# Single units at both ends of a fused recurrence and feed-forward: new weight pieces, output turns by transfer, and a re-planned order

## Chip, cores and metric

The kernel runs on one core of one Trainium2 chip. The metric is device time in microseconds (us). The comparison value is the median of several executions; one further execution was recorded by the hardware profiler, and its page and trace are what is read below. Engines: PE (TensorE), its weight loads (PEld), DVE (VectorE), ACT (ScalarE), POOL (GpSimd) and SP (SyncE, which only issues transfers).

## What is computed

```python
# q, k, v, alpha: (B=4, H=8, S=768, D=48) float32
for t in range(S):                       # one state per batch and head
    state = alpha[:, :, t, :, None] * state + einsum('bhd,bhe->bhde', k[:, :, t], v[:, :, t])
    y[:, :, t] = einsum('bhd,bhde->bhe', q[:, :, t], state)
x = y.transpose(0, 2, 1, 3).reshape(B * S, H * D)          # 3072 x 384
h = maximum(maximum(x @ w1, x @ w2), x @ w3)               # 3072 x 768
out = h @ w_out                                            # 3072 x 384
```

The setup draws alpha from 0.8 to 1.0.

## The kernel before, in words

The 768 positions are cut into 6 chunks of 128, and with 4 batches this gives 24 **units** (chunk, batch) of 128 positions and 8 heads; unit u is chunk u // 4, batch u % 4. Two neighbouring units are a **group** n; group n holds units 2n and 2n+1. The loads of q, k, v and alpha bring one tensor of one unit (192 KB) in the first four groups, later one tensor of a whole group (384 KB), into five rotating buffers each.

*Attention of one unit* (`decay`, `prep`, `output`, `state`): ACT takes the logarithm of alpha (L498). PE sums it along the chunk (L551, "cums") and forms the totals of the group (L511). ACT exponentiates with both signs (L554, L556). q and k are multiplied with these (L563) and v is scaled (L569 on ACT, L574 on POOL); the table EARLY names the engine of each of the three for some units, and POOL takes them for the rest. PE turns the products by 8 transposes (L533, "turn-in") and DVE copies them out (L537, tile qkT); from unit CROSS_IN on a transposing transfer on the SP queue does both (L581). PE makes the scores (L596), DVE masks them (L601, tile LA), PE makes the outputs (L639 with the carried state, L642 with the scores), ACT scales them (L650, tile xb). Three transposes (L664) and a copy (L668) give the turned output xT, or, from unit CROSS_OUT on, one transposing transfer on SP (L656; no unit has one before, since CROSS_OUT is 24). From unit PAIRS on the scores of two units are issued together. The state moves on by L694 (PE), L700 (DVE) and L707 (POOL, in the first chunk DVE).

*Feed-forward* (`ffn`): since max(a, b, c) = a + max(0, b - a, c - a), the kernel holds the differences w2 - w1 and w3 - w1 (tile wd, indexed by g = 0, 1; made by the subtractions of `subs`, L446) and the product w1 @ w_out (tile w1o; `turned`, L463, turns w1, and `folded`, L480, multiplies). A call serves two units. Six pieces of two 128-column blocks each are made for g = 0 and for g = 1 alternately: 6 matmuls of 256 columns (L735), then ACT's relu for g = 0 (L746) or DVE's maximum for g = 1 (L751), both into hT. Then "shrink" (L768), 9 matmuls of 384 columns for each unit: 3 of xT with w1o and 6 of hT with w_out. ACT copies the result out and issues the store (L779, L780).

*Weights* (`wload`) come over the SP queue in two pieces of 384 columns each (WCUTS); w1 and w_out are cast by ACT (L437). In the list FIRST, which fixes the order of the first transfers, ("w", g, p) is piece p of w1, w2, w3, w_out for g = 0, 1, 2, 3, and ("aq", n, 0, 1) the first unit of group n for alpha and q.

*Order.* The whole order is planned while the kernel is built. Each step has an engine, a cost, a rank and the tiles that it reads and writes. `Plan.order` takes again and again the step that can begin first, with ties by rank; it models the transfers (`Transfers`), PE's clock (`Clock`) and the eight PSUM banks. The instructions are emitted in that order, so each engine's queue is fixed before the run. The ranks of the feed-forward are its first unit plus LEAD. `warm` puts in matmuls of zeros (L676) at the lowest rank, which start behind one product of one unit (WARM).

Of the kernel before, what the change touches and what calls it, by code (L numbers as in the profile page):

```python
# [24 lines left out]
SP_FIRST = 0.9  # L25
QUEUES = ("SP", "POOL")
DMA_IN = {"SP": 0.9, "POOL": 2.7}
DMA_OUT = {"SP": 0.9, "POOL": 0.9}
DMA_BOTH = {"SP": 0.2, "POOL": 0.85}
SPARE = 1.5  # L30
LEAD = (6.0, 9.0, 7.0)
EARLY = {1: ("POOL", "DVE", "POOL"), 3: ("DVE", "DVE", "POOL"), 4: ("POOL", "POOL", "POOL"),
         5: ("DVE", "POOL", "POOL"), 6: ("DVE", "DVE", "POOL"), 7: ("POOL", "DVE", "POOL"),
         8: ("POOL", "DVE", "ACT"), 9: ("POOL", "DVE", "ACT"), 10: ("POOL", "DVE", "ACT"),
         11: ("POOL", "POOL", "POOL")}
WEIGHTS = ()
WCUTS = (0, 384, 768)
SUBS = {(1, 0): "DVE", (1, 1): "DVE", (2, 0): "DVE", (2, 1): "DVE"}
FIRST = (("aq", 0, 0, 1), ("aq", 0, 1, 2), ("k", 0, 1, 2), ("w", 0, 0), ("v", 1, 0, 1),
         ("k", 0, 0, 1), ("k", 1, 0, 1), ("w", 0, 1), ("qa", 1, 0, 1), ("w", 1, 1),  # L40
         ("w", 1, 0), ("v", 0, 0, 1), ("v", 0, 1, 2), ("k", 1, 1, 2), ("a", 1, 1, 2),
         ("w", 3, 1), ("q", 1, 1, 2), ("w", 3, 0), ("w", 2, 0), ("v", 1, 1, 2), ("w", 2, 1),
         ("aqkv", 2, 0, 2), ("a", 3, 0, 1), ("a", 3, 1, 2), ("qk", 3, 0, 1), ("v", 3, 0, 1),
         ("k", 3, 1, 2), ("q", 3, 1, 2), ("v", 3, 1, 2))
WARM = (0, 0, 12)
PAIRS, WIDE = 12, 99
CROSS_IN, CROSS_OUT = 21, 24
FETCH, FETCHES, STORE = 1.0, (24.5, 11.0), 0.3
CLOCK_WINDOW, CLOCK_PHASE, CLOCK_WAKE, CLOCK_KEEP = 3.413, 0.0, 0.75, 0.37

# [70 lines left out]
class Plan:  # L121
# [55 lines left out]
    def order(self):  # L177
# [16 lines left out]
        for i in range(n):  # L194
            if not waiting[i]:
                ready[i] = 0.0
                pending[self.steps[i][0]].add(i)
        free = dict(dict.fromkeys(HOP, 0.0), SP=SP_FIRST)
        bank_free = {b: 0.0 for b in range(NBANKS)}
        place, seq, clock = {}, [], Clock()  # L200
# [18 lines left out]
        while len(seq) < n:  # L219
            best = None  # L220
            for e, cand in pending.items():
                pick = None
                for i in cand:
                    at = self.homes(bank_free, self.steps[i][5])
                    if at is None:
                        continue
                    t = max(ready[i], free[e], at[0])
                    turn = TURN_RANK if e == "PE" and self.steps[i][7] != mode else 0.0
                    key = (t, self.steps[i][2] + turn, i)
                    if pick is None or key < pick:  # L230
                        pick = key
                if pick is not None and (best is None or pick < best[0]):
                    best = (pick, e)
# [4 lines left out]
            if landing and (best is None or landing[0] <= best[0][0]):  # L238
                end, i = dma.next(commit=True)
                self.landed[i] = end  # L240
                finish(i, end)
                continue
# [7 lines left out]
            if e == "PE":  # L250
# [3 lines left out]
                cost = clock.run(t, cost)  # L254
            free[e] = t + cost
            seq.append((t, i))
            if load and e in QUEUES:
                dma.add(e, t + cost + DMA_IN[e], load, i, late)
            else:
                if load:  # L260
                    dma.store(load)
                finish(i, t + cost + HOP[e])
# [7 lines left out]
def kernel(  # L270
# [111 lines left out]
    def banks2(key, dtype):  # L382
# [7 lines left out]
             (("a", alpha), ("q", q), ("k", k), ("v", v))}  # L390

    def load(n, lo, hi, names="aqkv"):
        cb, g = divmod(n, B // UB)
        for x in names:
            t = ld[x][n % 5]

            def run(x=x, t=t):
                nc.sync.dma_start(  # L398
                    t[:, lo:hi],
                    views[x][cb * P:(cb + 1) * P, g * HG + lo:g * HG + hi])  # L400

            plan.step("SP", 0.5, -1.0, run, line="loads",
                      writes=[(x, n % 5, h) for h in range(lo // H, hi // H)],
                      load=1.82 * (hi - lo) / HG,
                      late=0.0 if n < 3 else SPARE)

    nparts = len(WCUTS) - 1
    matrices = (moe_w1, moe_w2, moe_w3, moe_w_out)
    casting = {g: tuple(x[2] for x in FIRST if x[:2] == ("w", g)) for g in (0, 3)}

    def weights(g, gate):
        plan.step("POOL", 0.78, -1.0,
                  lambda: nc.gpsimd.dma_start((w1h, 0, 0, wo16)[g],
                                              matrices[g].rearrange("(t p) f -> p t f", p=P)),
                  reads=[gate], writes=[("w", g, p) for p in range(nparts)], line="weights",
                  load=3.2 if g == 0 else 4.1)
        if g == 0:
            turned()
        else:
            folded()  # L420

# [4 lines left out]
    def wload(g, part):  # L426
        plan.step("SP", 0.5, -1.0,
                  lambda: nc.sync.dma_start(  # L428
                      piece(wst[g], g, part),
                      piece(matrices[g].rearrange("(t p) f -> p t f", p=P), g, part)),  # L430
                  reads=[("ws room", p) for p in casting[0]] if g == 3 else [],
                  writes=[("ws", g, part)], line="loads",
                  load=3.25 * (WCUTS[part + 1] - WCUTS[part]) / DF)
        if g in (0, 3):
# [7 lines left out]
    def subs(g, part):  # L442
# [3 lines left out]
                  lambda: (nc.gpsimd if eng == "POOL" else nc.vector).tensor_sub(  # L446
                      wd[:, :, g - 1, cols], wst[g][:, :, cols], w1h[:, :, cols]),
                  reads=[("ws", g, part), ("w", 0, part)], writes=[("wd", g, part)])

# [41 lines left out]
    def decay(n):  # L491
# [28 lines left out]
        if cb > 0:  # L520
            m = n - B // UB
            plan.step("DVE", 0.45, 2 * n + 0.5,
                      lambda: nc.vector.tensor_mul(Gs[m % 3], e12s[m % 4][:, :, 1],
                                                   e12s[n % 4][:, :, 0]),
                      reads=[("e", m % 4), ("e", n % 4)], writes=[("G", m % 3)])

# [13 lines left out]
    def prep(u):  # L540
# [11 lines left out]

        plan.step("PE", 0.17, u, cums, banks=[Lk], reads=[("la", n % 3, i)], writes=[Lk])
        plan.step("ACT", 0.49, u, lambda: nc.scalar.activation(out=ep, in_=live[Lk], func=AFT.Exp),  # L554
# [4 lines left out]
        for w, x, e in ((0, "q", ep), (1, "k", en)):  # L559
# [3 lines left out]
                          nc.gpsimd if eng == "POOL" else nc.vector).tensor_mul(  # L563
                              qk[:, w, :, :D], ld[x][n % 5][:, hs], e),
                      reads=[(x, n % 5, i), ("ep" if w == 0 else "en", u % 3)],
                      writes=[("qk", u % 7, w)])
# [61 lines left out]
    def output(u):  # L628
# [6 lines left out]
        def outs():  # L635
            yp = live[yk] = bank(yk, [P, H, D], FP32)
            for j in range(NP):
# [3 lines left out]
                for p in range(2):  # L641
                    nc.tensor.matmul(yp[:, 2 * j + p, :], LA[:, p, j, :], v16[:, 2 * j + p, :],  # L642
                                     start=(cb == 0), stop=True, skip_group_check=True)

        plan.step("PE", 0.38 if cb else 0.21, u, outs, banks=[yk], writes=[yk],
                  reads=[("qkT", u % 3), ("LA", u % 3), ("v16", u % 7), ("qkT room", u % 3),
# [18 lines left out]

        plan.step("PE", 0.17, u, turn, banks=[xk], reads=[("xb", u % 5)], writes=[xk])
        plan.step("DVE", 0.35, u,
# [48 lines left out]
    def ffn(f, units):  # L716
# [3 lines left out]
        xT, hT = xTs[c][:, :, base * P:(base + k) * P], hTs[f % 3]  # L720
        span = 4 // k
        npieces = 2 * (NJ // span) + k
        rank = [u0 + LEAD[min(f, 2)] + k * i / npieces for i in range(npieces)]
        for q in range(NJ // span):
            js = range(q * span, (q + 1) * span)
            parts = sorted({p for j in js for p in parts_of(j // 2)})
            for g in range(2):
# [3 lines left out]
                def grow(js=js, g=g, gk=gk):  # L731
                    live[gk] = bank(gk, [P, span, k * P], FP32)
                    for jj, j in enumerate(js):
                        for kt in range(NFT):
                            nc.tensor.matmul(live[gk][:, jj, :], wd[:, kt, g, j * P:(j + 1) * P],  # L735
                                             xT[:, kt, :], start=(kt == 0), stop=(kt == NFT - 1))

                plan.step("PE", 0.656 if span > 1 else 0.643, r, grow, banks=[gk],
                          writes=[gk] + [("room", f % 3, j) for j in js] * (g == 0),
# [4 lines left out]
                if g == 0:  # L744
                    plan.step("ACT", 0.59, r,
                              lambda h=h, gk=gk: nc.scalar.activation(out=h, in_=live[gk],  # L746
                                                                      func=AFT.Relu),
                              reads=[gk], writes=[("hT", f % 3, j) for j in js])
                else:
                    plan.step("DVE", 0.69, r,  # L750
                              lambda h=h, gk=gk: nc.vector.tensor_max(h, live[gk], h),  # L751
                              reads=[gk] + [("hT", f % 3, j) for j in js],
                              writes=[("hT", f % 3, j) for j in js])
        for i in range(k):
# [4 lines left out]
            nk = NFT + NJ  # L759
            parts = [(0, nk)] if m < NU - UB else [(0, nk - 2), (nk - 2, nk)]  # L760
            for lo, hi in parts:
# [19 lines left out]

            plan.step("ACT", 0.86, r, leave, reads=[ok], writes=[("ob room", m % 4)], load=STORE)

# [12 lines left out]
    for n in range(NU // B):  # L796
        us = list(range(n * B, (n + 1) * B))
        due += [us] if n >= WIDE else [us[:UB], us[UB:]]
    nf = len(due)
    for n in range(NG):  # L800
# [6 lines left out]
        for u in range(n * UB, (n + 1) * UB):  # L807
# [3 lines left out]
            if u == WARM[0]:  # L811
                warm(*WARM)
            for g, after, x in WEIGHTS:
                if after == u:
                    weights(g, ("v16", u % 7) if x == "v" else ("qk", u % 7, "qk".index(x)))
            for v in (u - 1, u) if u >= PAIRS else (u,):
# [44 lines left out]
```

## Time and profile before

| what | before |
|---|---|
| median of 3 runs (lowest, highest) | 156.61 us (156.6, 157.32) |
| profiled execution: its time, its span | 157.07 us, 155.3 us |
| PE, PEld busy | 138.2 us (89%), 105.8 us (68%) |
| DVE, ACT, POOL busy | 100.6 us (65%), 86.5 us (56%), 67.2 us (43%) |
| read from HBM, written | 23.69 MB, 4.72 MB |
| last group's load issued | at 109.58 us |
| last matmul ends | at about 151.0 us |

The span runs from the first to the last recorded event; the run's own time is 1.77 us longer. Busy times of PE are unions of records whose ends are modelled and overlap, so PE's backlog is counted below by numbers of matmuls and their spacing in the chain of waits. The columns of that chain are: start in us, length in us, what it was.

### The profile page before, as it was taken

The page shows a single profiled execution, that of the slowest core. Times are in us where ns is not written, and L with a number is a line of the kernel's source. Part 1 is how long each engine was busy: PE and PEld are TensorE (multiplying, and loading weights), DVE is VectorE, ACT ScalarE, POOL GpSimd, SP SyncE. Part 2 cuts the span into 40 slices and gives each one's busy share as a digit, 9 for nine tenths or more (in the row PEclk, how much of TensorE's full clock was granted, in tenths as well). Part 3 has the DMA queues.
Part 4 walks back from the last instruction along what each step waited for, and adds up shares of the span by engine and source line. Part 5 has one row for each costly group of instructions (what it writes and reads, how often), then busy time and mean ns, then how long its engine had stood idle before and what let it go on. Part 6 is the DMA issues. An engine that isn't in the chain of part 4 may idle for free.

```text
span 155.3 us, 4013 instructions
## 1 busy us (share of the span) xinstructions
PE 138.2 (89%) x1600; PEld 105.8 (68%) x1600; DVE 100.6 (65%) x171; ACT 86.5 (56%) x173; POOL 67.2 (43%) x95
## 2 busy tenths in 40 slices
PE   0578537999998999999999999999999999999990
PEld 0244425757777967798778688878797787868750
DVE  7044756398599997669768869958684752923220
ACT  3734707747547666496768284848575462535221
POOL 0332190011912154076999749999858600000000
PEclk9999999999999999999999999999999999999999
DMA  6999999999999999999999999999894232011202
GB/s 123 227 240 253 325 209 344 330 181 232 207 243 219 180 239 246 211 269 189 231 219 207 222 253 231 180 243 267 195 202 86 101 72 77 24 55 51 83 18 101
DMA packets 109394, 29.45 MB, mean 190 GB/s; under 512 B 103104, under 2 KB 109376, under 8 KB 109376
## 3 DMA queue, kind: packets, MB, share of 16 engines
q1 hardware_dynamic: 105632, 24.38, 75.4%
q10 hardware_dynamic: 3744, 4.82, 9.1%
q8 instruction: 12, 0.20, 0.5%
q14 instruction: 6, 0.05, 0.1%
HBM read 23.69 MB, written 4.72 MB: 183 GB/s over the span
## 4 chain that ended last, share of the span: by engine, by line
PE 76%; SPq 6%; issue 4%; DVE 4%; DMA 3%; POOL 2%; ACT 2%; ACTq 0%; POOLq 0%
PE psum L735 30%; PE psum L768 23%; PE psum L533 5%; SPq L398 5%; PE psum L596 4%; DMA qn<-in_q_dram 3%; PE psum L642 3%; PE psum L639 2%; POOL qk L563 2%; PE psum L551 2%; PE psum L664 2%; PE psum L480 2%; PE psum L694 2%; DVE LA L601 2%; SPq L428 1%
## 5 line engine op out<-in xcount | busy, mean ns | idle before, releaser
L735 PE MATMUL psum<-xT,wd 128*128 128x256 f16 x432 | 55.7, 276 | 0.2
L735 PEld LDWEIGHTS <-wd 128*128 128x128 f16 x432 | 41.0, 99 | 7.1 <-issue 0.5
L563 POOL TENSOR_TENSOR qk<-qn,ep 128x384 f16<-128x384 f32 x21 | 21.5, 1028 | 37.5 <-ACT ep L554 29.7
L751 DVE TENSOR_TENSOR hT<-psum,hT 128x512 f16<-128x512 f32 x36 | 24.2, 686 | 16.0 <-PE psum L735 12.1
L601 DVE TENSOR_TENSOR LA<-psum,c 128x1024 f16<-128x1024 f32 x24 | 28.6, 1216 | 7.0 <-PE psum L596 7.0
L746 ACT ACTIVATE hT<-psum 128x512 f16<-128x512 f32 x36 | 21.5, 605 | 17.2 <-PE psum L735 16.9
L768 PE MATMUL psum<-wo,hT 128*128 128x384 f16 x144 | 27.3, 326 | 0.0
L779 ACT COPY ob<-psum 128x384 f32<-128x384 f32 x24 | 11.5, 478 | 23.2 <-PE psum L768 22.8
L768 PEld LDWEIGHTS <-hT 128*128 128x128 f16 x144 | 14.1, 98 | 9.3
L650 ACT ACTIVATE xb<-psum,c 128x384 f16<-128x384 f32 x24 | 13.9, 582 | 10.7 <-PE psum L642 9.6
L574 POOL TENSOR_SCALAR v<-vn,c 128x384 f16<-128x384 f32 x21 | 12.6, 601 | 13.7 <-DMA vn<-in_v_dram 13.5
L563 POOL TENSOR_TENSOR qk<-kn,en 128x384 f16<-128x384 f32 x17 | 18.4, 1087 | 0.2 <-DMA kn<-in_k_dram 0.2
L537 DVE COPY qkT<-psum 128x1024 f16<-128x1024 f16 x21 | 14.2, 685 | 5.7 <-PE psum L533 5.0
L533 PE MATMUL psum<-c,qk 128*128 128x128 f16 x168 | 14.5, 232 | 3.8 <-POOL qk L563 3.7
L707 POOL TENSOR_TENSOR Z<-U,G 48x192 f16<-48x192 f32 x32 | 15.7, 504 | 3.9 <-DVE U L700 2.8
L768 PE MATMUL psum<-w1o,xT 128*128 128x384 f16 x72 | 15.7, 326 | 0.0
L533 PEld LDWEIGHTS <-qk 128*128 128x128 f16 x168 | 11.2, 104 | 5.7 <-POOL qk L563 4.6
L554 ACT ACTIVATE ep<-psum 128x384 f32<-128x384 f32 x24 | 11.9, 495 | 2.8 <-PE psum L551 2.7
L668 DVE COPY xT<-psum 128x384 f16<-128x384 f16 x24 | 8.3, 352 | 7.7 <-PE psum L664 6.5
L551 PE MATMUL psum<-la,c 128*128 128x384 f16 x24 | 8.5, 354 | 4.5 <-ACT la L498 4.5
L498 ACT ACTIVATE la<-an 128x768 f16<-128x768 f32 (+1 forms) x15 | 10.7, 711 | 2.8 <-DMA an<-in_alpha_dram 1.4
L556 ACT ACTIVATE en<-psum 128x384 f32<-128x384 f32 x24 | 12.0, 501 | 0.0
(40 smaller groups left out, 155.0 us busy)
## 6 DMA issues: line engine op xcount, KB each, us to landing
out_dram<-ob ACTq DMA_DIRECT2D x24, 192.0 KB, 3.0
ws<-in_moe_w_dram SPq DMA_DIRECT2D x6, 576.0 KB, 5.9
an<-in_alpha_dram SPq DMA_DIRECT2D x9, 384.0 KB, 6.1
qn<-in_q_dram SPq DMA_DIRECT2D x9, 384.0 KB, 6.1
kn<-in_k_dram SPq DMA_DIRECT2D x9, 384.0 KB, 5.3
vn<-in_v_dram SPq DMA_DIRECT2D x9, 384.0 KB, 5.8
an<-in_alpha_dram SPq DMA_DIRECT2D x6, 192.0 KB, 4.6
qn<-in_q_dram SPq DMA_DIRECT2D x6, 192.0 KB, 4.2
```

Source lines behind the costliest of these rows:

```text
L533: nc.tensor.transpose(live[tk][:, w, j, :], qk[:, w, 2 * j:2 * j + 2, :], ident)
L537: plan.step("DVE", 0.69, u, lambda: nc.vector.tensor_copy(out=qkT, in_=live[tk]), reads=[tk], writes=[("qkT", u % 3)])
L556: plan.step("ACT", 0.49, u, lambda: nc.scalar.activation(out=en, in_=live[Lk], func=AFT.Exp, scale=-1.0), reads=[Lk], writes=[("en", u % 3)])
L563: nc.gpsimd if eng == "POOL" else nc.vector).tensor_mul(
L574: lambda: nc.gpsimd.tensor_scalar(out=v16, in0=ld["v"][n % 5][:, hs], scalar1=vsc, scalar2=1.0, op0=AOP.mult, op1=AOP.mult),
L601: lambda: nc.vector.tensor_mul(LA.rearrange("p a b t -> p (a b) t"), live[Ak].rearrange("p a (b t) -> p (a b) t", t=P), maskA.unsqueeze(1) ...
L650: lambda: nc.scalar.activation(out=xb, in_=live[yk].rearrange("p a b -> p (a b)"), func=AFT.Copy, scale=ysc),
L707: eng.tensor_mul(Zn[rows, :, cols], U[rows, :, cols], G[rows, i * NP:(i + 1) * NP].unsqueeze(2).broadcast_to([D, NP, D]))
L735: nc.tensor.matmul(live[gk][:, jj, :], wd[:, kt, g, j * P:(j + 1) * P], xT[:, kt, :], start=(kt == 0), stop=(kt == NFT - 1))
L746: lambda h=h, gk=gk: nc.scalar.activation(out=h, in_=live[gk], func=AFT.Relu),
L751: lambda h=h, gk=gk: nc.vector.tensor_max(h, live[gk], h),
L768: nc.tensor.matmul(live[ok], a[:, i * P:(i + 1) * P], w, start=(kt == 0), stop=(kt == nk - 1))
```

## The change

The first four and the last two units get a feed-forward call of their own (SINGLE, LAST); such a call has four pieces of three blocks, each of 9 matmuls of 128 columns. The weights come in pieces of 256 and 512 columns. The turned outputs of units 18 to 23 come by transfers (CROSS_OUT 24 to 18); the products q, k of unit 21 are turned by PE again (CROSS_IN 21 to 22). Scores are paired from unit 10 instead of 12. The list of first transfers is new: the tensors of the first four units ahead of nearly all weights. The zero matmuls are 21 instead of 12 and start behind the q product of unit 2 instead of that of unit 0. Two of the four subtractions go from DVE to POOL, and EARLY is new. The last unit's output is copied and stored in two halves. The planner gets finer costs, a model of DVE and POOL holding each other up, and a limit on transfers in flight; all of these act on the time only through the order.

```diff
-LEAD = (6.0, 9.0, 7.0)
-EARLY = {1: ("POOL", "DVE", "POOL"), 3: ("DVE", "DVE", "POOL"), 4: ("POOL", "POOL", "POOL"),
...
-WCUTS = (0, 384, 768)
-SUBS = {(1, 0): "DVE", (1, 1): "DVE", (2, 0): "DVE", (2, 1): "DVE"}
-FIRST = (("aq", 0, 0, 1), ("aq", 0, 1, 2), ("k", 0, 1, 2), ("w", 0, 0), ("v", 1, 0, 1),
-         ("k", 0, 0, 1), ("k", 1, 0, 1), ("w", 0, 1), ("qa", 1, 0, 1), ("w", 1, 1),
-         ("w", 1, 0), ("v", 0, 0, 1), ("v", 0, 1, 2), ("k", 1, 1, 2), ("a", 1, 1, 2),
-         ("w", 3, 1), ("q", 1, 1, 2), ("w", 3, 0), ("w", 2, 0), ("v", 1, 1, 2), ("w", 2, 1),
...
-WARM = (0, 0, 12)
-PAIRS, WIDE = 12, 99
-CROSS_IN, CROSS_OUT = 21, 24
...
+LANES, LANES_USED, LANDING = {"SP": 6, "ACT": 99}, 2, 2.4
+LEAD = (7.5, 6.0, 6.0, 7.5)
+EARLY = {0: ("DVE", "DVE", "ACT"), 2: ("POOL", "POOL", "ACT"), 4: ("DVE", "POOL", "ACT"),
+         5: ("POOL", "POOL", "POOL"), 6: ("DVE", "POOL", "POOL"), 9: ("POOL", "POOL", "ACT"),
+         10: ("POOL", "DVE", "ACT")}
+WCUTS = (0, 256, 768)
+SUBS = {(1, 0): "POOL", (1, 1): "DVE", (2, 0): "DVE", (2, 1): "POOL"}
+FIRST = (("a", 0, 0, 2), ("v", 0, 0, 1), ("qv", 1, 1, 2), ("v", 0, 1, 2), ("k", 0, 1, 2),
+         ("a", 1, 0, 1), ("vk", 1, 0, 1), ("q", 1, 0, 1), ("q", 0, 1, 2), ("a", 1, 1, 2),
+         ("w", 0, 0), ("k", 0, 0, 1), ("w", 0, 1), ("k", 1, 1, 2), ("q", 0, 0, 1), ("w", 1, 1),
+         ("w", 3, 0), ("w", 3, 1), ("w", 1, 0), ("w", 2, 1), ("a", 2, 0, 1), ("w", 2, 0),
...
+WARM = (2, 0, 21)
+BACK, WQUEUE, WTAX = 1, "SP", 0.1
+SINGLE, LAST = 4, 2
+PAIRS, WIDE = 10, 99
+CROSS_IN, CROSS_OUT = 22, 18
...
+                    if e == "POOL" or e == "DVE" and self.steps[i][7]:
+                        t = max(t, held["DVE" if e == "POOL" else "POOL"])
+                    if self.steps[i][6] and len(lanes) >= LANES[e]:
...
-        span = 4 // k
+        span = (3, 2, 0, 1)[k - 1]
...
-            parts = [(0, nk)] if m < NU - UB else [(0, nk - 2), (nk - 2, nk)]
+            parts = [(0, nk)] if m < NU - UB else [(0, nk - span), (nk - span, nk)]
...
-            plan.step("ACT", 0.86, r, leave, reads=[ok], writes=[("ob room", m % 4)], load=STORE)
+            if m < NU - 1:
+                plan.step("ACT", 0.86, r, leave, reads=[ok], writes=[("ob room", m % 4)], load=-STORE)
+                continue
+            left, right = slice(0, DM // 2), slice(DM // 2, DM)
...
+            def leave_left(m=m, ok=ok, rows=rows):
+                nc.scalar.copy(out=obs[m % 4][:, left], in_=live[ok][:, left])
+                nc.scalar.dma_start(rows[:, left], obs[m % 4][:, left])
...
+            plan.step("DVE", 0.3, r,
+                      lambda m=m, ok=ok: nc.vector.tensor_copy(out=obs[m % 4][:, right],
+                                                               in_=live[ok][:, right]),
+                      reads=[ok], writes=["right"])
+            plan.step("SP", 0.4, r,
+                      lambda m=m, rows=rows: nc.sync.dma_start(rows[:, right],
+                                                               obs[m % 4][:, right]),
...
+    due = [x for us in due for x in ([[u] for u in us] if us[0] < SINGLE or us[0] >= NU - LAST
+                                     else [us])]
```

## The prediction

> **What bounds the kernel now.** First the page's slices of the span: the rows are busy tenths of PE and of the transfers in 40 slices of 3.88 us.
>
> ```profile
> PE   0578537999998999999999999999999999999990
> ...
> DMA  6999999999999999999999999999894232011202
> ```
>
> The transfers are full from the second slice to the thirtieth (116 us). PE is nearly full from the eighth slice on (27 us). So PE sets the end, and the transfers set when PE can start. The chain of waits shows the hand-over:
>
> ```profile
> 10.60 4.92 DMA qn<-in_q_dram
> 15.56 3.13 issue
> 18.73 3.68 POOL qk L563 x2
> ...
> 27.05 2.64 PE psum L735 x12
> ...
> 33.94 0.66 PE psum L735 x6
> ...
> 42.52 0.45 PE psum L533 x8
> ```
>
> Twelve matmuls of 256 columns take 2.64 us at 27.05 (0.22 each), six take 0.66 at 33.94 (0.11 each): PE runs at half rate until about 29.7, although the clock row of the page shows 9 throughout. PE's timeline shows what raised it: two dense stretches of 3.6 us (6.8 to 10.4 and 11.2 to 14.8) did not, the dense 5.8 us from 23.84 did.
>
> Spacings at full rate in the chain: L735 0.109, L768 0.163, a 128-column transpose 0.056; per unit scores 0.28, outputs 0.38 (0.21 in the first chunk), cums 0.163, state 0.17; totals 0.18 a group. After 35 us the groups of PE count 408 L735 (44.6 us), 216 L768 (35.1), 136 L533 and 63 L664 (11.1), 20 units' scores (5.5), outputs (7.5), cums (3.3), states (3.4), 10 totals (1.8) and 6 folds (1.0): **113.3 us of work in the 116.0 us** to the last matmul at 151.0. So 2.7 us are stalls and turns. Ahead of 35 us PE did only about 10.9 us of work (24 L735 2.6, 12 folds 2.0, 32 turn-ins 1.8, 18 w1 turns 1.0, attention outputs, scores, cums and totals 3.5). Everything that can be got: more work ahead of 35, fewer stalls after it, a shorter end. The end:
>
> ```profile
> 148.40 2.61 PE psum L768 x16
> 151.01 0.02 issue
> 151.03 0.49 ACT ob L779
> 151.52 0.02 issue
> 151.54 0.34 ACTq L780
> ...
> 151.98 0.48 ACT ob L779
> ```
>
> Both last units' results leave one behind the other: 4.3 us from the last matmul to the span's end at 155.3.
>
> **The end, part by part.** With calls of their own, unit 22 leaves some 3.5 us ahead of unit 23 (18 blocks of matmuls and 9 L768), so its copy and issue (151.03 to 151.98: 0.95) leave the chain. The last copy is halved: ACT's 512 columns take 0.605 and 384 take 0.478, so 0.001 a column, and 192 columns some 0.29 instead of 0.48: -0.2. DVE copies the other half beside it (384 columns of float16 take 0.35) and SP issues in 0.45, the least of its row; the halves finish within 0.2 of each other. Sum **-1.1** (bounds -1.3 and -0.7, if SP's half is late by 0.4).
>
> **PE's work.** Six turns by PE fewer (3 L664, 0.167 each): -1.0, and DVE loses six copies of 0.352. One turn-in more (unit 21): +0.45, DVE +0.69. Units 10 and 11 paired: 0.55 for 0.66, -0.1. Six single units: 216 matmuls of 128 columns for 108 of 256. The nearest row is the turn-in above, 128x128 with a new weight load each, 8 in 0.45: 216 x 0.056 = 12.0 for 11.8, **+0.2**. The row's weight loads last 104 ns and still hide; the other end, each load (99 ns in the L735 row) showing in full, is +9.6, and less is no possibility since the columns are the same. I take 0.056, the row of the same shape. Sum **-0.4**.
>
> The Trainium skill, "TensorE: Matmul & The Clock Gate", section "Back-to-back issue gap", gives about 81 ns a matmul for streams of load and matmul with 128 columns. By that rule the sum would be +5.7 for the singles, not +0.2; the row of 8 in 0.45 here speaks against it.
>
> ACT and DVE read 4 pieces of 384 columns for a single pair's two units and did 3 of 512: 1.92 for 1.8 and 2.24 for 2.06 by the same slopes. Neither is full (56%, 65%), so nothing.
>
> **The transfers by PE's turn.** A transposing transfer of qkT took 3.1 to 4.7 us to land; xT is 3/8 of its columns, so between that and nothing, against 0.8 for turn and copy: at most +4 in one unit's latency. In the trace the turns of units 22 and 23 (135.66, 137.29) are needed at 141.5 or later, so it is covered. If the cover is gone, PE waits up to 4 us at one place. On SP's queue each stands behind the loads: the last load is issued at 109.58, the turn of unit 18 comes at 115.44, so no load waits for it; only other transfers of this kind do. The store of the last right half waits on SP with nothing behind it.
>
> **The start.** Landings: the first alpha tensor at 3.84 (0.74 + 3.1), the last weight piece at 33.1 (24.95 + 8.2), with 15 tensors of 192 KB and 8 weight halves between: at 0.9 a tensor (three of 384 KB land 1.85 to 2.9 apart around 36 to 41) a half is 1.98, so 1.32 for 256 columns and 2.64 for 512. Along the new list: unit 2 complete at 12.8, unit 1 at 13.7, first weight piece 15.9, all of w1 19.5, units 3 and 0 complete at 20.4 and 21.3, w2 columns 256 to 767 at 23.9, w_out 27.9, rest of w2 29.2, w3 31.8 and 34.1. **The bytes ahead of the last w3 piece are the same plus one tensor (+0.9)**; what changes is what can be done before it.
>
> The zero matmuls start behind unit 2's q product (12.8 + 1.0 to 1.6 on POOL: about 14.5). Seven took 2.45, so 21 take some 7 us. That is longer than the 5.8 that sufficed and twice the 3.6 that didn't: PE should be at full rate by about 21.5 instead of 29.7. Their wait is new on PE's queue: behind it stand unit 2's own turn-in, which needs the same product, and the turns of w1, which can't begin before 16.7 (15.9 and the cast); so nothing is late by it, and the same zeros, as filler, take at most one matmul (0.33) from real work.
>
> Work open to PE ahead of 35 then: attention of four units (1.3 each, 5.3), totals 0.4, w1 turned 1.0, folded 2.9 from 29.4 on, all of g = 0 for four units (72 x 0.056 = 4.0; the 512-column part from 25.7, after DVE's 1.8 subtraction by the 1.36 for 1152), four states 0.7: 14.3, against 10.9. The other part of g = 0 waits for POOL's subtraction of 768 elements. No row has one; POOL's product of 384 takes 1.03, and 1.60 to 2.10 beside DVE's subtractions at 18.7, so 2.1 to 4.2, ending 31.3 to 33.4. I take the lower end, since little runs on DVE there, and let 0.9 slip past 35: **-2.5** (bounds -3.4 and 0).
>
> POOL's other subtraction, 1536 elements of w3, is 4.1 to 8.4 by the same row: 35.9 to 40.2, with the products of units 4 and 5 behind it. Till then PE has the other half of g = 1 (2.0) and after it the shrinks (5.9); at the long end it waits 2 to 3 us.
>
> **Stalls after 35.** A new order makes new ones. Named now: 46 to 52 and 90 to 95. I take no change; bounds -2 and +3.
>
> **Sum:** -1.1 - 0.4 - 2.5 + 0 = -4.0: span 151.3, the profiled time 157.07 to 153.1, the median 156.61 to **152.6**.
>
> **The rivals.**
> - *Start given back*: PE is ahead at 35 but units 4 to 7, whose loads still land between 35 and 48, aren't ready when the first four are used up. For: the transfers are full, and their bytes are the same. Against: at 35 the four units leave 9.9 us, and units 4 and 5 are due at about 45. Only end and work remain: -1.5, **155.1**. Chance 0.16.
> - *All of it and fewer stalls*: -1.1 - 0.4 - 3.4 - 1.9: **149.8**. For: DVE loses 1.4 net, the planner counts engines that hold each other up. Chance 0.12.
> - *The order doesn't fit the chip*: POOL's long subtraction or a late transfer makes 4 us of new stalls: **156.6**. This is also the case that the change doesn't do what it says. Chance 0.07.
> - *Slower: weight loads of the singles show.* 144 of the 216 matmuls may lie on the full stretch (the 72 of g = 0 at the start lie in idle time); at 99 ns instead of 56 they cost 6.2: **158.8**. It decides from 4.0 / 144 + 0.056 = 0.084 us a matmul. Against: 168 turn-ins of that shape hide theirs. Chance 0.07.
>
> By the Trainium skill's 81 ns this last one would cost 3.6 and end near 156.2, level with before.
>
> Forecast: 0.58, with its own range 151 to 154.3. The range for 8 in 10 takes in the bounds of start and stalls: from the rival at 149.8 to 155.5, a little beyond the one at 155.1. About 0.5% (0.8 us) is what a measurement can tell from no change: faster 0.86, same 0.07, slower 0.07.
>
> **What would show it.** Right: 12 or so L735 at half rate gone, 0.5 for nine from about 22; more than 13 us of PE work ahead of 35; one ACT copy of 192 columns behind the last matmul and 3.2 us to the end. Wrong: nine L735 of a single unit over 0.7 us; PE waiting for POOL's L446 or for a load between 36 and 50; PE waiting for an xT transfer near the end; half rate again after 22.

## Result and the profile after

| | before | after |
|---|---|---|
| median of 4 runs (lowest, highest) | 156.69 us (156.60, 157.32) | 154.66 us (153.41, 155.54) |
| profiled execution: its time, its span | 157.07, 155.3 us | 155.54, 153.8 us |
| last matmul ends; from there to the span's end | 151.0; 4.3 us | 150.4; 3.4 us |
| PE work ahead of 35 us, behind it (counted by spacing) | 11.1, 113.3 us | 9.9, 114.1 us |
| stalls of PE from 35 us to its last matmul | 2.7 us | 1.3 us |

The change is faster, by 2.0 us in the medians: a ratio of 0.988 with the 95% interval 0.983 to 0.993, so clear of noise but only 1.2%. Forecast were 152.6 us and a ratio of 0.974. Measured again on two chips, the changed kernel gave 0.981 (0.975 to 0.988) and 0.979 (0.974 to 0.984). The profiled execution is the longest of the four; two of the others, at 153.41 and 153.78 us, lie in the forecast's own range of 151 to 154.3, the median doesn't. The ratios leave out runs over 1.5% above a kernel's fastest; the changed kernel's runs spread by more than that, so the medians of all runs stand beside them below.

The page's slices, in the order of the prediction (PE, transfers):

```profile
PE   0211949999999999999999999999999999999991
...
DMA  6999969998998999999999999999992562122121
```

PE has fewer gaps from the eighth slice on, and does less ahead of it; the transfers are as full as before, with one dip in the sixth slice. The chain of waits (start, length, what) of the start:

```profile
13.60 7.50 DMA ws<-in_moe_w_dram
21.12 1.48 ACT w1h L448
22.64 1.46 PE psum L475 x12
...
27.83 1.04 issue
28.88 1.76 DVE wd L457
30.68 1.18 PE psum L748 x18
...
35.62 0.50 PE psum L748 x9
```

The first feed-forward matmul (now L748, its subtraction L457) stands at 30.68 us; it was at 27.05 (L735). It hangs on the large piece of w1, which took 7.5 us to land. Behind its cast PE, in the planned order, turns w1, then unit 0's products; DVE masks their scores, and only then subtracts. PE's part of this chain, from 22.64 to 27.65, lasts 5.0 us, most of it at half rate. The end:

```profile
148.93 1.48 PE psum L781 x9
150.40 0.02 issue
150.43 0.33 ACT ob L802
150.75 0.02 issue
150.78 0.36 DVE ob L808
```

Unit 22's copy and issue have left the chain. The two halves follow each other: by the trace DVE's copy waited 1.2 us, and the last that it waited for was ACT's copy.

### The profile page after: what moved, and what is told of

Same layout as the page of the kernel before. It is cut to its first block, busy times and chain, and to the rows that moved or that the text cites. A ratio compares the mean times of both kernels' runs of the same rounds, so it can differ in the third digit from the quotient of the medians.

```text
span 153.8 us, 4257 instructions
## 1 busy us (share of the span) xinstructions
PE 135.0 (88%) x1707; PEld 106.1 (69%) x1707; DVE 95.0 (62%) x163; ACT 88.0 (57%) x178; POOL 74.1 (48%) x100
## 4 chain that ended last, share of the span: by engine, by line
PE 81%; SPq 8%; DMA 5%; DVE 1%; issue 1%; ACT 1%; DVEq 0%
PE psum L748 31%; PE psum L781 23%; SPq L416 7%; PE psum L545 6%; DMA ws<-in_moe_w_dram 5%; PE psum L609 4%; PE psum L655 3%; PE psum L563 2%; PE psum L652 2%; PE psum L707 2%; PE psum L677 2%; PE psum L492 2%; PE psum L523 1%; DVE wd L457 1%; ACT w1h L448 1%
## 5 line engine op out<-in xcount | busy, mean ns | idle before, releaser
L748 PE MATMUL psum<-xT,wd 128*128 128x256 f16 (+1 forms) x540 | 54.6, 251 | 0.1
L748 PEld LDWEIGHTS <-wd 128*128 128x128 f16 x540 | 42.9, 98 | 5.2 <-DVE wd L457 0.3
L764 DVE TENSOR_TENSOR hT<-psum,hT 128x512 f16<-128x512 f32 (+1 forms) x39 | 24.7, 646 | 16.0 <-PE psum L748 9.8
L575 POOL TENSOR_TENSOR qk<-kn,en 128x384 f16<-128x384 f32 x22 | 22.6, 1027 | 15.9 <-ACT en L568 9.1
L759 ACT ACTIVATE hT<-psum 128x512 f16<-128x512 f32 (+1 forms) x39 | 21.6, 571 | 14.1 <-PE psum L748 13.7
L781 PE MATMUL psum<-wo,hT 128*128 128x384 f16 x144 | 27.5, 326 | 0.0
L575 POOL TENSOR_TENSOR qk<-qn,ep 128x384 f16<-128x384 f32 x21 | 20.8, 999 | 12.1 <-ACT ep L566 11.2
L549 DVE COPY qkT<-psum 128x1024 f16<-128x1024 f16 x22 | 14.9, 687 | 17.4 <-PE psum L545 16.6
L545 PEld LDWEIGHTS <-qk 128*128 128x128 f16 x176 | 11.8, 104 | 9.0 <-POOL qk L575 8.2
L587 POOL TENSOR_SCALAR v<-vn,c 128x384 f16<-128x384 f32 x19 | 11.4, 601 | 9.0 <-DMA vn<-in_v_dram 8.7
L566 ACT ACTIVATE ep<-psum 128x384 f32<-128x384 f32 x24 | 11.8, 493 | 3.7 <-PE psum L563 3.0
L655 PE MATMUL psum<-v,LA 128*128 128x48 f16 x192 | 11.3, 186 | 0.1
```

The costliest lines, as they stand in the source:

```text
L545: nc.tensor.transpose(live[tk][:, w, j, :], qk[:, w, 2 * j:2 * j + 2, :], ident)
L549: plan.step("DVE", 0.69, u, lambda: nc.vector.tensor_copy(out=qkT, in_=live[tk]), reads=[tk], writes=[("qkT", u % 3)])
L781: nc.tensor.matmul(live[ok], a[:, i * P:(i + 1) * P], w, start=(kt == 0), stop=(kt == nk - 1))
```

## Experiments

Unless said otherwise the planned order is kept as it is, by moving, adding or taking out single steps behind the planning. "Base" is the changed kernel. Differences in us are of the median of all runs to the kernel before's in the same group; for the base they were -2.0, -1.8 (`again`) and -3.1 (`again2`), -2.3 in the mean. Numbers like 0.983, 0.979 to 0.988 are the ratio to the kernel before and its 95% interval. PE's work and stalls are counted from each run's trace as in the table above.

**The base repeated** (`again`, `again2`: no edit).

> The changed kernel once more, to see the spread of its runs: the first four were 155.5, 153.4, 153.8 and 155.5 us. Theory A (PE's full rate begins at a different point of the start from run to run, about 26.5 us in the first trace, and the masks and the subtraction behind it move with it): runs again fall in two groups some 2 us apart, and the trace of a run near 153.5 shows full rate ahead of 24 us and the first L748 ahead of 29.5. Theory B (the spread comes from the transfers): the groups differ in when tensors land, by over 1 us at 33, with full rate at the same time.

> The changed kernel a third time, as the common yardstick of this group: ratio to before 0.98 to 0.99, spread some 2 us.

Measured: medians of 155.78 against 157.59 before, and 153.74 against 156.88. The trace of `again` is of its longest run (156.85). The two traces differ by 3.8 us in their spans (155.1 and 151.3). The chain of waits of `again2`:

```profile
13.38 6.03 DMA ws<-in_moe_w_dram
19.44 1.48 ACT w1h L448
20.97 1.46 PE psum L475 x12
...
26.44 1.76 DVE wd L457
28.24 1.18 PE psum L748 x18
```

The same transfer, issued 0.2 us earlier than in the first trace, landed 1.7 us earlier, and the last piece of w3 at 32.9 instead of 34.9 (35.1 in `again`). PE's last matmul ended **119.73 us behind the first L748** in all three traces (30.68 and 150.41; 31.98 and 151.71; 28.24 and 147.97). PE was at full rate from about 26.6, 28.9 and 23.1. Theory B, the transfers, fits a part: w1's large piece landed at 21.1, 21.6 and 19.4, and that is 2.2 of the 3.7 us by which the first L748 moved. The rest lies behind the landing: the first L748 followed it by 9.6, 10.3 and 8.8 us, in the order in which full rate came. So Theory A isn't excluded.

**Zeros and PE's half rate** (`gap_filled`, `no_zeros`).

```diff
+    for _ in range(6):                     # gap_filled
+        plan.steps.append(("PE", 0.163, 90.0, warm_run))
+        seq.insert(at, len(plan.steps) - 1)    # at: place of the second turn of w1
...
+    seq = [i for i in seq if plan.steps[i][3].__name__ != "zeros"]   # no_zeros
```

> Six more matmuls of zeros (1.96 us at half rate) stand where PE waited 2.1 us for the cast of w1, 20.5 to 22.6 us; nothing else moves. Theory A: PE is dense from 14.6 on, full rate comes by 23 us in every run, the turns, scores and masks of units 0 and 3 run up to 1.5 us earlier, and all runs are near 153.6 (-1 us in the median, no second group). Theory B: nothing changes, within 0.3 us.

> The changed kernel without its 21 matmuls of zeros, order kept. By the prediction they bring full rate 8 us earlier and the start depends on it. The traces put their worth lower: full rate came at 26.6 and 28.4, and what followed waited for weights. Theory A: without them PE is at half rate until 32 to 34, L748 and the folds there take twice as long, 1 to 2 us slower. Rival (the weights set the pace, PE has room): within 0.5 us.

Measured: 155.24 (-2.4; 0.985, 0.979 to 0.990) with the gap filled, 153.95 (-2.9; 0.983, 0.979 to 0.988) without any zeros. PE's timeline shows the clock's part: in `gap_filled` the turns of w1 ran at full rate at 23.16, in the base of the first trace at half rate.

```profile
23.16 0.91 PE L475 MATMUL psum<-c,w1h 128*128 128x128 f16 x12
```

```profile
22.64 1.46 PE L475 MATMUL psum<-c,w1h 128*128 128x128 f16 x12 [2.12 <-ACT w1h L448]
```

Without zeros the first feed-forward matmuls begin at half rate, at 27.85 against 28.24 in `again2`:

```profile
27.85 1.75 PE L748 MATMUL psum<-xT,wd 128*128 128x128 f16 x18
```

Yet work ahead of 35 us (12.2) and time are as in `again2` (12.4). So the zeros as they stand are worth nothing in the time, and Theory A of `no_zeros` falls. In both runs the chain of waits no longer goes over PE's stretch behind w1's cast: it goes over the landing of w_out's first piece (25.30 without zeros, 27.75 with the gap filled) and ACT's cast of it, and the first L748 came 8.0 and 8.6 us behind w1's landing. A faster PE there meets this next limit. The filled gap was partly lost again: work ahead of 35 us was 11.2, stalls after it 2.9 us, most of the excess between 100 and 120.

**SP's wait and DVE's order** (`own_stage`, `sub_early`). w_out's staging moves into the fifth buffers of the loads, made as one tile; or the subtraction and 18 matmuls move ahead.

```diff
-        wst[3] = wst[0].rearrange("p t f -> p (t f)").rearrange("p (t f) -> p t f", f=DM)
+        wst[3] = wide[:, :3].rearrange("p x h d -> p (x h d)").rearrange("p (t f) -> p t f", f=DM)
...
+    move(87, 65)        # w2's large subtraction ahead of unit 0's turn copy
+    move(279, 114)      # first pieces of units 1 and 2
+    move(332, 114)
```

> w_out is staged in the buffers of the fifth group's loads, still empty then, and not in w1's staging buffer; the order is the same on every engine. SP no longer waits for w1's cast from 20.98 to 22.61 us. If that wait cost transfer time (theory C): w_out, the rest of w2 and w3 land some 1.0 to 1.6 us earlier (w3's last piece at 33.3 to 33.9 instead of 34.85) and the median falls by up to 1.2 us. Rival: the transfers are as full without it, landings move by under 0.4 us and the time stays within 0.4 us.

> Order kept, except that DVE's subtraction for the 512-column piece of w2 stands ahead of unit 0's turn copy (its data landed at 24.9 us, it ran at 28.9 behind a mask), and the two first-half pieces of units 1 and 2 (18 matmuls, 1.0 us) stand ahead of unit 0's outputs. Theory D (order on DVE, not the data, held the first feed-forward work back): subtraction at about 25, these matmuls from 28.0 instead of 30.7, end of PE's work and median earlier by 0.7 to 1.2 us. Rival (PE is behind on other work, what is done earlier only moves idle time): within 0.4 us.

Measured: 154.99 (-2.6) and 155.83 (-1.8), against -1.8 of the base in the same group. With its own staging w3's last piece landed at 33.2, first L748 29.11, last matmul 148.84: again 119.73 behind. The median moved 0.8, less than the spread of the runs. In `sub_early` the 18 matmuls did run at 26.99, but the next L748 came at 31.70 and the last matmul at 150.13: only idle time was moved. Theory D falls.

**Both, and the middle's loads** (`start_both`, `start_both2`, `both_thin`, `alpha_ahead`, `before_thin`, `spare4`). The first two join `own_stage` and `gap_filled`; the others add one edit each, `before_thin` on the kernel before.

```diff
+                if x == "v" and n >= 5:     # both_thin, before_thin
+                    return
...
+    for g in range(7):                      # alpha_ahead
+        move(loads[4 * g + 4], loads[4 * g + 3])
...
-SPARE = 1.5                                 # spare4, planned anew
+SPARE = 4.0
```

> The last two start edits together, order kept: w_out staged apart and six more zeros in the gap. The traces so far: work of PE done ahead of 35 us is 11.1 before, 9.9 and 8.6 in two traces of the changed kernel, 11.5 with the own staging, 11.2 with the filled gap. Here some 12.5 is due, and if the start alone sets the end (theory S), PE's last matmul comes about 1.5 to 2.5 us earlier than in the repeated changed kernel. Theory E (PE, once ahead, catches up with the loads in the middle: alpha of a group was used 0.0 us after its landing in six of eight groups with the filled gap): half or more of it is given back as stalls after 35 of 2.5 us or more, and the median is within 1.2 us of the repeated changed kernel.

> As the run before this one, and the loads of v from the sixth group on are left out (seven transfers of 384 KB; the products then use the v of an earlier group, so this part of the computation is another one). All instructions of PE, DVE, ACT and POOL stay. Theory E: with the middle's transfers a quarter shorter no alpha is waited for, stalls after 35 us are 1.3 or less, and the median falls by 1 to 2.5 us against the run before. Theory S: transfers in the middle are covered, stalls and time stay within 0.5 us.

> Own staging and filled gap again, beside the changed kernel on the same chip. The trace showed 12.5 us of work ahead of 35 (9.9 in the changed kernel) and 3.3 us of stalls after it (1.3). Theory E: 0.4 to 1.2 us faster than the changed kernel. Theory S (all of the start reaches the end): 2 us or more. Rival: no difference over 0.3 us.

> As the run before this one, with one move on SP's queue in each of the last seven groups: the next group's alpha ahead of the group's own v. All other orders are the same. Theory E (alpha, the first tensor used, lands just in time): alpha lands about 2 us earlier against its use, stalls after 35 fall by 1 us or more, the median by 0.5 to 1.5 us. Rival (v, now 2 us later, or q and k are as late: all four are just in time): stalls move to POOL's v and the products, time within 0.4 us or slower.

> The kernel before, without the loads of v from the sixth group on (its products use the v of an earlier group, so this part of the computation is another one). Theory E for the kernel before: its middle waits too where the transfers are slow, so it gains 0.5 to 1.5 us, and keeps the stall of 1.0 us at 45 to 50, where PE waits for a turned output and not for a load. Rival: its middle has cover, under 0.4 us.

> The changed kernel with own staging and filled gap, planned with 4.0 us instead of 1.5 us of lateness for the loads from the fourth group on, so that more feed-forward work is placed ahead of each group's attention; the order of the start stays, nothing else changes. Theory E (the order of the middle has no spare time for its loads): alpha is used 2 us or more after its landing in most groups, stalls after 35 us fall from 3.3 to 1.8 or less, the median falls by 0.7 to 1.8 us against the run without it and the spread of the runs (153.1 to 155.6) narrows. Rival (the stalls are only moved to the end, since PE's last work waits for the last load): stalls and time within 0.4 us.

| run | median, difference | work ahead of 35 | stalls after it |
|---|---|---|---|
| start_both | 154.87, -2.4 | 12.5 | 3.3 |
| both_thin | 154.46, -2.8 | 11.2 | 1.3 |
| start_both2 | 153.97, -2.9 | 12.5 | 1.5 |
| alpha_ahead | 154.28, -2.6 | 13.3 | 2.0 |
| before_thin | 156.85, +0.1 | 10.6 | 3.3 |
| spare4 | 160.02, +3.3 | 11.7 | 7.5 |

Beside `again2` the joint edits bring nothing in the time (153.97 to 153.74), though the first L748 came only 7.7 us behind w1's landing in both their traces. In some executions the middle does wait: `start_both` shows 3.3 us of stalls, 1.9 of them from 70 to 100, where alpha is used at its landing; with the loads of v left out they are gone. But alpha landing 2.3 to 4.5 us ahead of its use in the middle (`alpha_ahead`) doesn't move the median, and the kernel before gains nothing from fewer loads. So Theory E names an occasional loss, not the missing gain. `spare4` did put 4 to 8 us between landing and use, and its runs lie close (159.7 to 160.9), but PE then waits for scaled outputs and turns (2.9 us between 60 and 70 alone): the price of lateness in the plan is far above its worth.

**Parts of the change** (`before_tail`, `before_cross`, `old_start`, `no_single`).

```diff
-        span = 4 // k                       # before_tail, on the kernel before, with the halved store
+        span = (3, 2)[k - 1]
+    due = [x for us in due for x in ([[u] for u in us] if us[0] >= NU - 2 else [us])]
...
-CROSS_IN, CROSS_OUT = 21, 24                # before_cross, on the kernel before
+CROSS_IN, CROSS_OUT = 22, 18
...
-SINGLE, LAST = 4, 2                         # no_single; old_start: also LEAD, EARLY, WCUTS, SUBS, FIRST, WARM of before
+SINGLE, LAST = 0, 2
```

> The kernel before with only the end of the change: calls of their own for the last two units and the last store in halves; the order ahead of about 138 us is the same. If the end's term was right (3.4 us from the last matmul to the span's end instead of 4.3): 0.8 to 1.1 us faster than before. Rival: the single units' matmuls or the wait for hT cost it, under 0.4 us.

> The kernel before with only the turns moved: outputs of units 18 to 23 by transfers, products of unit 21 by PE; order the same until about 112 us. By the working of the prediction 0.55 us of PE work goes: 0.4 to 0.6 us faster. Rival: a turned output comes late, PE waits: equal or slower, with a wait of PE behind a transfer between 112 and 148.

> The changed kernel with the start of before (list of first transfers, pieces of 384 columns, engines of the products, zeros, ranks; the first four units in pairs), planned anew. If the new start gains nothing by itself (work ahead of 35 us 9.9 against 11.1 before) and the gain is the end and fewer stalls, this is as fast as the changed kernel within 0.8 us, or faster by up to 1. If the new start is what gains, it falls back to within 1.2 us of before.

> The changed kernel with the first four units in pairs (SINGLE = 0), planned anew from the first feed-forward on; the transfers, weights and zeros of the start stay. Theory F (the single calls fill PE at 45 to 60 us, where the kernel before stalls): stalls of 1 us or more come back between 35 and 60, and the time rises by 0.7 to 1.5 us against the changed kernel. Rival (the new list of transfers does it, or the gain is the plan's later order): within 0.5 us of the changed kernel.

Measured: `before_tail` 156.63 (-0.7; 0.994 to 0.999) with 3.4 us from last matmul to end; `before_cross` 156.10 (-0.6; 0.994 to 1.000); `old_start` 156.89 (-0.4; 0.993 to 0.999), stalls 3.4; `no_single` 156.00 (-0.7; 0.990 to 0.998), stalls 2.6, its trace from a run of 157.54. So the end is worth some two thirds of its -1.1, and the turns what was reckoned, though their interval just reaches no change. Without the new start and the single calls together 1.9 us of 2.3 are gone, without the single calls alone 1.6. So what shows is the single calls with the order planned around them; the new list of transfers, weight pieces and zeros account for 0.3 by this, which is within the noise. Nor do the parts add up: `old_start` keeps end and turns, -1.3 by themselves, and shows -0.4. Both were planned anew, and their later order differs too. Work ahead of 35 us doesn't tell them apart (10.5 in `old_start`, 9.9 in the base's first trace). The stalls came back, in `no_single` at 60 to 80 (1.4 us) and not at 35 to 60 as Theory F had it, so its place is not confirmed.

**Bytes ahead of the first feed-forward** (`extra_load`, `less_load`).

```diff
+    plan.steps.append(("SP", 0.5, -1.0, again_a))          # extra_load: 384 KB of alpha, group 4
+    seq.insert(seq.index(12), len(plan.steps) - 1)         # ahead of w1's first piece
...
+    nc.vector.memset(ld["v"][1], 0.0)                      # less_load
...
+    seq = [i for i in seq if i not in (3, 7)]              # the fourth and the eighth transfer
```

> The changed kernel with one more transfer of 384 KB (1.8 us by the tensors' pace) ahead of w1's first piece, into a buffer that is empty then and written again later; all else kept. In four executions of this order PE's last matmul came 119.73 us behind the first L748, which moved from 28.2 to 32.0 with the landing of w1's large piece (19.4 to 21.7). Theory T (the start's transfers set the end, one for one): first L748 and end 1.3 to 2.0 us later than in the changed kernel, ratio to before 0.99 or more. Rival (the start has cover, PE's work does not): within 0.5 us, ratio 0.98 to 0.985.

> The changed kernel without the two loads of v for units 2 and 3 (192 KB each, the second and fourth to ninth in the list); zeros are written there once instead, so this part of the computation is another one. Theory T: w1's large piece lands some 1.8 us earlier, first L748 and end 1.0 to 1.8 us earlier, ratio to before 0.97 to 0.975. Rival: within 0.5 us, ratio 0.98 to 0.985.

Measured: 156.27 (-0.4; 0.998, 0.995 to 1.001) and 151.40 (-5.3; 0.965, 0.961 to 0.968): +1.9 and -3.0 us against the base's mean; against each of the base's three differences +1.4 to +2.7 and -2.2 to -3.5. w1's large piece landed at 22.3 and 17.6, the first L748 stood at 31.33 and 25.56, and the last matmul 119.73 and 119.72 us behind. PE's timeline of `less_load`, from the turns of w1 to the first feed-forward matmuls:

```profile
19.11 1.10 PE L476 MATMUL psum<-c,w1h 128*128 128x128 f16 x12
...
25.56 1.18 PE L749 MATMUL psum<-xT,wd 128*128 128x128 f16 x18
```

**Theory T is borne out**: 384 KB ahead of w1, 1.8 us of transfer, move the end both ways, later by about as much, earlier by more. For the excess the trace of `less_load` has a reason: PE reached full rate within the turns of w1 (12 in 1.10 us, 1.46 at half rate), so its part of the chain took 3.4 us, from 19.11 to 22.52, instead of 5.0, and the first L748 came 8.0 us behind w1's landing. This run also has two tensors less to wait for in its products; that share isn't separated.

## Why the prediction fell short

- *The end*, -1.1: the traces show -0.9, alone on the kernel before -0.7. Unit 22's copy and issue are gone from the chain as reckoned; the halved copy gained nothing of its 0.2, since DVE's half follows ACT's (0.33 and 0.36 for one copy of 0.48).
- *PE's work*, -0.4: 124.4 to 124.0 by count. Nine 128-column matmuls take 0.50 (35.62 in the chain above): 0.056 each as taken, so the slower rival falls. The 81 ns of the Trainium skill ("TensorE: Matmul & The Clock Gate", "Back-to-back issue gap") don't hold for this stream.
- *The transfers by PE's turn*: four of the six xT transfers landed in 2.3 us; the first took 4.0, and 5.8 in `again2`, more than the 4.7 reckoned as the most. No wait of PE for one shows.
- *The start*, -2.5: **this step failed.** 13.4 us of PE work ahead of 35 were reckoned; three traces of the base show 9.9, 8.6 and 12.4, against 11.1 before. There are four errors in it.
  1. The landings were one execution's pace taken as fixed: all of w1 at 19.5 and w3 at 34.1 were met in `again2` (19.4 and 32.9), but came at 21.1 and 34.9 in the compared profile, and `extra_load` and `less_load` show that this goes through to the end.
  2. The first g = 0 matmuls were put behind their own data (25.7); in the order they stand behind unit 0's whole attention on PE and DVE, at 28.2 to 32.0; `sub_early` shows that this alone cost nothing at the end.
  3. The working counted 0.7 us of states ahead of 35, although they need the decay of the next chunk, whose alpha landed at 33.6.
  4. Full rate was due by 21.5 and came at 26.6. The dense stretch of 5.8 us that the working read as sufficient holds an idle 0.38 us at 25.40, so it was no measure; in the changed kernel PE was dense for 5.9 us from 14.63 without a rise; and the zeros didn't stand together, 3 of the 21 came before 20.5 us, the rest as filler behind 24.2.

  Along the chain the late landing (21.1 for 19.5) and the half rate (5.0 us for 3.4) make 1.6 us each, 3.2 of the 3.7 us between the forecast -2.5 and the +1.2 of this trace; this is an estimate from the two traces, no run separates them. The subtractions on POOL took 1.65 and 3.10 us; the lower ends that the prediction took from the product's row, 2.1 and 4.1, were too high.
- *Stalls*, 0: no change was forecast; 1.3 to 1.4 us remain of 2.7 in every trace of the base. The kernel before loses 1.1 us at 45 to 50, where PE waits for a turned output behind DVE's state updates; in the changed kernel 0.1 us is lost there. That the single calls cause it is argued: `no_single` bears it out in time, not in place.

The trace of `again2` adds up to the forecast by other terms: start -1.3, work -0.4, stalls -1.3, end -1.0, and its span is the 151.3 us forecast; but 1.3 of it comes from stalls, which were forecast to stay, and the start gave half of its 2.5: that is luck. The compared execution had the later landings: start +1.2, and -1.5 in all. That is the number of the rival "start given back", and luck too: its mechanism, waits between 36 and 50, isn't there (0.2 us of stalls).

The Trainium skill ("TensorE: Matmul & The Clock Gate", Part 1: The HAM clock gate) has the clock rise after a busy window of about 3.4 us that is free-running, so at a varying point. Here it rose at 23.1, 26.6 and 28.9 in one order. In `again2` PE stayed at half rate from 14.63 to 23.1 with only 0.35 us idle in all, longer than two such windows (6.8 us, an estimate from the page's figure); which of its work there counts as busy, no run here shows.

Left open: why the same first transfers take up to 2 us longer in some executions; what PE's half rate alone costs at the start, since every run that changed it moved another limit too; and whether the early loads of v for units 2 and 3, put later instead of left out, would keep part of the 3 us; this was not tried.

## What to carry over

Where PE's order runs without slack from its first dense work to the end, what happens before that point sets the time: count the bytes ahead of it, ask which of them it truly needs, and look at the rate of PE on the chain behind them. A gain in work done early has to be checked against the queue order and against the spread of landings of more than one execution, not against one trace's pace. Stalls that an order avoids can be worth as much as the work that it moves: here 1.4 us by the traces.

## What had not been expected of the hardware

Seven of eleven executions with equal order behind the start kept 119.72 to 119.73 us from the first feed-forward matmul to the last, while the start moved by over 6 us; the other four took 119.91 to 121.88, with stalls in the middle (`gap_filled`, `start_both`) or a first piece at half rate (`no_zeros`, 120.29). One transfer of 768 KB landed 6.0 to 7.6 us after its issue in three executions of one kernel. The clock row shows 9 in all 40 slices of the kernel before while matmuls run at half rate (12 of 256 columns in 2.64 us at 27.05, against 6 in 0.66 at full rate at 33.94). It isn't blind to the rate: in `old_start`, where PE was at full rate at 11.8 us (6 turns in 0.51) and at half again at 27.5 (12 in 2.74), it shows 5 from the sixth to the eighth slice (19.4 to 31.0). In these traces it is the half rate at the very start that doesn't show; the spacing of equal matmuls tells it.
